# A gated recurrence and a squared-ReLU layer in one program: another order of the opening, shorter zero products, a later third step of each weight conversion, narrower state products in the last blocks

## The chip, the core and the metric

The kernel runs on one core of one Trainium2 chip. The metric is the device time of one execution in microseconds; lower is better. A core has a matrix engine (TensorE, PE in the profile, with its weight loads listed as PEld), a vector engine (VectorE, DVE), a scalar engine (ScalarE, ACT), GpSimd (POOL) and a queue engine (SyncE, SP) that here issues all transfers. Each engine works through its own list of instructions in order and waits on semaphores for the others.

## What is computed

Per head and batch, a state of 48 x 48 is decayed row by row with alpha and takes up the outer product of k and v; q reads it. The results, side by side by head, go through two matrix products with a squared ReLU between them. All is float32, except the two weight matrices, which arrive as float64 bit patterns.

```python
batch, n_heads, seq, head_dim = (4, 8, 768, 48)
for t in range(S):
    state = alpha[:, :, t, :, None] * state + np.einsum('bhd,bhe->bhde', k[:, :, t], v[:, :, t])
    y[:, :, t] = np.einsum('bhd,bhde->bhe', q[:, :, t], state)
x = y.transpose(0, 2, 1, 3).reshape(B * S, H * D)      # 3072 x 384
h = np.maximum(x @ w_in, 0.0)                          # w_in 384 x 2048
return (h * h @ w_out).astype(np.float32)              # w_out 2048 x 384
```

## The kernel before

**Blocks and groups.** The sequence is cut into 6 chunks of 128 steps; a block is one chunk of one batch, all 8 heads: 24 blocks, numbered chunk by chunk, so that blocks 0 to 3 are the first chunk of the four batches. Four blocks make a group of 512 rows for the two layers: 6 groups.

**One block of the recurrence.** `ln` takes the logarithm of alpha (ScalarE), `cs` sums the logs along the chunk with a triangular matrix (TensorE), `eb` and `ei` take the exponentials of the sums and their negatives (ScalarE), `mq` and `mk` scale q and k with them (VectorE). q and k are turned (`qT`, `kT` in the first group, `turn` later, L351 and L567) and copied to SBUF by ScalarE (`qc`, `kc`). `scores` (L410) multiplies turned k and q in four quarters of 64 x 64; `masked` (L421) copies the causal part. `state_sums` (L438) multiplies k and v, the k times v products; `sums_copied` (L451) adds the first half's sums to the state, and `next_state` (L467, L468) makes the new state and decays it by the last row of the exponentials, which `lt` brings into columns (L334, L341; later a transfer does it). y is made for two blocks at a time from the states and from the masked scores (L390, steps `ya`, `yb`), and `ev` (L605) copies it from PSUM into x, some copies on VectorE (those listed under `evd`), the rest on ScalarE. Each head has 48 columns in a slot of 64; the pad columns of k are zero, so the k times v product with 64 columns of k writes zeros into rows 48 to 63 of its slot.

**The layers.** `ffn_in` (L908) multiplies w_in and x for one of 16 columns blocks j of the hidden layer, in float32, which counts as two TensorE instructions a product in the trace; a whole unit has 3 products with 512 rows, a half unit (`ha`, `hb`) 3 with 256, the first or the last two blocks of the group. From group 1 on, most products are made in three passes with rounded parts of the operands (L715 and L798), whose splits VectorE and ScalarE prepare. After the last pass of a hidden column block the squared ReLU is made in one of three kinds, chosen by j modulo 4 from a string of letters: A (three operations on ScalarE), M (two on ScalarE, one on VectorE), D (one on ScalarE, two on VectorE).

**Weights.** w_in and w_out come in 8 slices each of 768 KB (w0, w1 and so on). A slice is converted in seven operations: two on VectorE (`convert_first`, L163 and L167), two on ScalarE (`convert_middle`, L177 and L180), three on VectorE (`convert_second`, L188, L192, L195). Four raw slices can be held. A transfer of q, k, v or alpha is 192 KB.

**The order.** The scheduler keeps the order in which the program records its operations on each engine. The opening is a written list of words in `AT['first']`, run one by one (`ln0` is the step `ln` for block 0; `load2a` loads alpha of block 2, `weights0` the next raw slice; `first0`, `middle0`, `second0` convert slice 0). Before it, `AT['pre']` lists the first six loads. `warm` and `zeros` are TensorE products with zeros that nobody reads. After the list, the units of the layers are laid in a row, each with a cost in plan units, and events (conversions, steps of later blocks, splits) are put between them at due times from `AT` (`weave`, the last lines). In `attention`, the due times of a pair of blocks follow from one number per pair in `AT['g0']`, `AT['g1']` and `AT['g']`.

Of the kernel before, what the change touches and what calls it, by code (L numbers as in the profile page):

```python
# [9 lines left out]
FP32 = mybir.dt.float32  # L10
# [3 lines left out]
ALU = mybir.AluOpType  # L14
# [1 line left out]


GB = 4
AT = {'later': (0, 0, 5, 4, 0, 1, 1), 'evs': 0.5, 'lead': 4, 'post': 3, 'w_first': (46.75, 40.5, 50.75), 'wstep': 1.4, 'w_in_at': 2.25, 'w_in_by': 3.6, 'room1': 22, 'room': 24, 's0': 4, 'ahead': 6, 'late': 2, 'xs': 0.05, 'g0': ((-0.25, 4, False, True, 25.5), (22.25, 6, True, True), (28.25, 8, True, False)), 'sc0': (2.45, 2.35, 2.35), 'g1': ((4.5, 8, False, 16.25), (14.25, 10, True), (34.75, 12, True)), 'g': ((2.075, 6, True), (14.25, 8, True)), 'g1x': 52.0, 'gx': 48.25, 'g0x': 55.75, 'k0': 2, 'h0': 17, 'k1': 4, 'h1': 0, 'h1by': 2, 'evs0': 0.5, 'tp': 'ADMD', 'tp1': 'ADAD', 'split': 8, 'o0': (47.5, 46.75), 'o1': (), 'o2': (22.0, 26.25, 25.25, 38.5, 39.75, 35.0), 'str1': 19.5, 'ga': 9.75, 'gb': 12.5, 'cv0': 0.875, 'pre': '0a 1a 0q 0k 1q 1k', 'cp': (), 'evd': ((0, 1, 0), (0, 1, 2), (2, 0, 2), (2, 1, 0), (2, 1, 1), (2, 1, 2), (2, 1, 3)), 'first': 'ln0 warm0 ln1 cs0 zeros3 ei0 mk0 eb0 mq0 kT0 cs1 load2a qT0 kc0 load0v eb1 qc0 sc0 mq1 ei1 ln2 weights0 qT1 am0 qc1 kv0 mk1 load1v first0 kT1 us0 kc1 lt1 sc1 load2q load2k kv1 load3a am1 cs2 eb2 us1 ei2 middle0 ya0 yb0 load2v mk2 ln3 mq2 qT2 qc2 kT2 load3k cs3 ep00 ep01 load3q ep02 load3v kc2 lt0 weights1 sc2 eb3 kv2 second0 ei3 ep03 zeros3 first1 weights2 lt2 middle1 ha0 load4q mk3 mq3 qT3 am2 kT3 qc3 kc3 ha1 sc3 lt3 st0 kv3 load4k second1 am3 us2 ha2 us3 load4a ya2 first2 yb2 weights5 ep20 ep21 weights3 ha3 weights6 ep22 ep23 weights4 middle2 second2 st3 st2 hb2 st1 load4v hb3 hb0 hb1'}


RUN = {0: 128, 32: 32, 64: 64, 96: 32}
# [3 lines left out]
def kernel(  # L26
# [12 lines left out]
    nc = tc.nc  # L39
    B, H, S, D = q.shape  # L40
    C = 128
    NCH = S // C
    NP = H // 2
# [4 lines left out]
    G = 64 - D  # L48
# [19 lines left out]
    s_t = [s_all.pop(0) for _ in range(B)]  # L68
# [8 lines left out]
    NW = 8  # L77
# [21 lines left out]
    def tile_of(x, n):  # L99
        return lent.get((x, n), tiles[x][n % len(tiles[x])])  # L100
# [4 lines left out]
    given, owner = set(), {}  # L105
# [37 lines left out]
    half = {}  # L143
# [35 lines left out]
        )  # L179
        nc.scalar.activation(out=w, in_=lo, func=AF.Copy, scale=2.0**-52, bias=1.0)  # L180

    def convert_second(i):
        if moe_w_in.dtype == FP32:
            return
        need(("mid", i))
        given.add(("w", i))
        w, lo, hi, power, upper = half.pop(i)
        nc.vector.scalar_tensor_tensor(  # L188
            out=power, in0=hi, scalar=0x80000000, in1=power,
            op0=ALU.bitwise_and, op1=ALU.bitwise_or,  # L190
        )
        nc.vector.scalar_tensor_tensor(  # L192
            out=w, in0=upper, scalar=2.0**-20, in1=w, op0=ALU.mult, op1=ALU.add
        )
        nc.vector.tensor_tensor(out=w, in0=w, in1=power.bitcast(FP32), op=ALU.mult)  # L195

    for word in AT["pre"].split():
        load(int(word[0]), word[1:])
# [25 lines left out]
    last = consts.tile([128, 4, NP], FP32, name="last")  # L224
# [18 lines left out]
    blk = [{} for _ in range(NBLK)]  # L243
# [17 lines left out]

    SPLIT = AT["split"]

# [98 lines left out]
    def copied(x, n):  # L362
        t = blk[n][f"{x}s"] = work(f"{x}s", 2 if x == "k" else 4)
        copy = nc.vector.tensor_copy if f"{x}{n}" in AT["cp"] else nc.scalar.copy
        copy(out=t, in_=blk[n].pop(f"{x}T"))
# [8 lines left out]
    def zeros(n):  # L374

        ps = bank(n, "zeros", (2 * NP, 64))
        for _ in range(3):
            nc.tensor.matmul(  # L378
                out=ps[:, 0:NP, :], lhsT=s_t[3].rearrange("a p d -> a (p d)")[:, 0:128],
                rhs=s_t[3], start=True, stop=True,  # L380
            )

    def y_begin(n):
# [16 lines left out]
    HALF = [slice(0, 64), slice(64, C)]  # L400
# [29 lines left out]
    def state_sums(n):  # L430
        need(("v", n), ("kb", n))
        given.add(("free", "k", n))
        ps = two[n]
        for p in range(NP):
            for e in range(2):
                first = (2 * p + e) * D
                for h in range(1 if n // B == NCH - 1 else 2):
                    nc.tensor.matmul(  # L438
                        out=ps[h][64 * e : 64 * (e + 1), 1, p, G:64],
                        lhsT=tile_of("k", n)[HALF[h], 2 * p + e, :],  # L440
                        rhs=tiles["v"][n % NV][HALF[h], first : first + D],
                        start=True, stop=True, skip_group_check=True,
                    )

    def sums_copied(n):

        if n >= 3:
            need(("st", n - 3), ("y", n - 3))
        ps = two.pop(n)
        u = blk[n]["u"] = u_all[n % 3]  # L450
        nc.vector.tensor_tensor(  # L451
            out=own(u), in0=own(ps[0][:, 1]), in1=own(s_t[n % B]), op=ALU.add
        )
        blk[n]["kv1"] = own(ps[1][:, 1])

    def own(x):
        return x[:, :, G:64]

    def next_state(n):
        blk[n]["s"] = s_t[n % B]  # L460
        given.add(("st", n))
        if n // B < NCH - 1:
            need(("last", n))
            s_all.append(s_t[n % B])
            s_t[n % B] = s_all.pop(0)
            s, last = own(s_t[n % B]), last_t[n % 4].unsqueeze(2).to_broadcast([128, NP, D])
            nc.vector.tensor_tensor(out=s, in0=blk[n].pop("kv1"), in1=own(blk[n]["u"]), op=ALU.add)  # L467
            nc.vector.tensor_tensor(out=s, in0=s, in1=last, op=ALU.mult)  # L468

    def dep(later, earlier):  # L470
        tc.add_manual_dep(
# [113 lines left out]
    def ev(n, ps=tuple(range(NP))):  # L585
# [12 lines left out]
        for p in ps:  # L598
            for e, f, end in ((1, 2 * p * D + 32, 2 * (p + 1) * D), (0, 2 * p * D, (2 * p + 1) * D)):
                copy = nc.vector.tensor_copy if (n, e, p) in AT["evd"] else nc.scalar.copy  # L600
                r = 64 * (e ^ p % 2)
# [28 lines left out]
    here, todo, room = {}, [], [22]  # L630
# [8 lines left out]
    late = [False]  # L639
# [20 lines left out]
    def diff_w(w, p):  # L660
# [7 lines left out]
        for x in "ld":  # L668
            t = made.pop((x, w, p))
            if w == "i" or p >= NW - AT["k0"] or (x == "l" and p >= NW - AT["k1"]):  # L670
                here[x, w, p] = t
        pump()

    def prepare(at, w, p):
        step = AT["wstep"]
        fs = (cast_w, rest_w, diff_w)
# [289 lines left out]
    first = AT["first"]  # L966
# [127 lines left out]
    units.append((0, ended, (0,)))  # L1094
    base = [0]
    cv0 = AT["cv0"]
    events = [(3.4 * i + cv0, next_weights, (3 + i,)) for i in range(-3, 2 * NW - 3) if ("mid", 3 + i) not in given]
    events += [(3.4 * i + cv0 + 1.5, convert_second, (3 + i,)) for i in range(-3, 2 * NW - 3) if ("w", 3 + i) not in given]
    events += [(0, load, (GB + 1,)), (1.0, load, (GB + 2, "k"))]
    for p, at in enumerate(AT["w_first"]):  # L1100
        events += prepare(at, "i", p)
# [7 lines left out]
    for g in range(1, NG):  # L1109
# [11 lines left out]
        if g == 1:  # L1121
            m = len(AT["w_first"])
# [4 lines left out]
            n = min(AT["k0"], AT["k1"])  # L1127
# [34 lines left out]
```

## Time and profile before

| what | value |
|---|---|
| median of 3 runs | 523.61 us (522.96 to 523.86) |
| the profiled execution: its own time | 523.38 us |
| its span | 521.6 us |
| TensorE busy | 511.3 us (98%) |
| VectorE busy | 363.7 us (70%) |
| ScalarE busy | 304.8 us (58%) |
| mean granted TensorE clock | 0.997 |
| transfers | 102.35 MB, 196 GB/s on average |

The span is the profiled execution from its first to its last instruction; the time of the execution has 1.8 us more around it. Busy shares are averages over stages with different limits: the opening, in which attention of the first blocks and the first weight slices arrive, is bound by other things than the stream behind it. "Idle before" in a line is the time that the engine stood still just before these instructions, with what ended most of it. The chain of waits follows the end of the program back from instruction to what released it. The mean duration of a small TensorE product (221 ns) is its latency; several run at once, so the pace is read from the length of a whole piece.

### The profile page before, as it was taken

To read this page: it belongs to the slowest core of one execution; us is meant where nothing else is said; L and a number is where in the kernel's file an instruction comes from. 1 tells how busy PE (TensorE), PEld (TensorE's weight loads), DVE (VectorE), ACT (ScalarE), POOL (GpSimd) and SP (SyncE) were. 2 spreads that over 40 slices of the span, in tenths; PEclk is the share of its full clock that TensorE was granted. 3 is DMA by queue.
4 is the path that set the end of the run, shared out by engine and by line. 5 is a ranking of instruction groups with operands and counts; after the bars stand their busy time and mean duration, and the time that the engine had idled before them with its cause. 6 is when DMAs were issued, how large, how long until landed. Compare 5 with 4: busy or idle time off the path is not lost.

```text
span 521.6 us, 13021 instructions
## 1 busy us (share of the span) xinstructions
PE 511.3 (98%) x5340; PEld 422.0 (81%) x5340; DVE 363.7 (70%) x628; ACT 304.8 (58%) x649; POOL 5.3 (1%) x29
## 2 busy tenths in 40 slices
PE   8799999999999999999999999999999999999997
PEld 6675455669888669987899988899988899988997
DVE  3577989999886958866587477487465386363861
ACT  4658895577778834585773275872275683164620
POOL 4000000000000000000000000000000000000000
PEclk9899999999999999999999999999999999999999
DMA  9997878556587675999784678864683544699201
GB/s 185 185 284 157 235 190 185 115 130 237 187 234 173 199 218 165 286 310 246 179 239 153 214 246 221 231 197 142 207 284 128 175 129 152 208 389 299 74 1 60
DMA packets 139323, 102.35 MB, mean 196 GB/s; under 512 B 109808, under 2 KB 112896, under 8 KB 139264
## 3 DMA queue, kind: packets, MB, share of 16 engines
q1 hardware_dynamic: 139264, 101.52, 68.4%
q8 instruction: 42, 0.69, 0.6%
q14 instruction: 17, 0.14, 0.1%
HBM read 84.17 MB, written 17.33 MB: 195 GB/s over the span
## 4 chain that ended last, share of the span: by engine, by line
PE 94%; SPq 2%; ACT 1%; DMA 1%; DVE 1%; issue 0%; POOLq 0%; DVEq 0%
PE o L798 41%; PE h L715 32%; PE h L908 7%; PE y L390 5%; PE sckv L410 2%; PE T L567 2%; PE sckv L438 2%; SPq L119 1%; DMA v_in<-in_v_dram 1%; PE cs L280 1%; PE cs L283 1%; PE cs L284 1%; PE zeros L378 1%; DVE x L605 0%; ACT x L605 0%
## 5 line engine op out<-in xcount | busy, mean ns | idle before, releaser
L715 PE MATMUL h<-xd,wd 128*128 128x512 f32 x240 | 68.4, 397 | 0.5 <-issue 0.5
L715 PE MATMUL h<-xa,wb 128*128 128x512 f32 x240 | 68.6, 394 | 0.0
L715 PE MATMUL h<-xl,wl 128*128 128x512 f32 x240 | 67.7, 390 | 0.0
L637 DVE TENSOR_TENSOR hid<-h,hid 128x512 f32<-128x512 f32 x40 | 27.6, 689 | 54.0 <-PE h L715 53.9
L605 ACT COPY x<-y 16x256 f32<-16x256 f32 (+2 forms) x133 | 46.9, 365 | 22.6 <-PE y L390 18.8
L732 ACT ACTIVATE h<-h 128x512 f32<-128x512 f32 x40 | 23.3, 582 | 56.6 <-PE h L715 56.3
L798 PE MATMUL o<-wb,ha 128*128 128x384 f32 x160 | 54.4, 340 | 0.0
L798 PE MATMUL o<-wd,hd 128*128 128x384 f32 x304 | 53.7, 334 | 0.0
L798 PE MATMUL o<-wl,hl 128*128 128x384 f32 x160 | 53.6, 335 | 0.0
L798 PE MATMUL o<-w_out,hid 128*128 128x384 f32 x160 | 53.6, 489 | 0.0
L715 PEld LDWEIGHTS h<-xl,wl 128*128 128x128 f32 x240 | 45.1, 188 | 9.8
L798 PEld LDWEIGHTS o<-wd,hd 128*128 128x128 f32 x304 | 52.8, 188 | 0.0
L715 PEld LDWEIGHTS h<-xd,wd 128*128 128x128 f32 x240 | 44.1, 188 | 9.9 <-issue 0.9
L715 PEld LDWEIGHTS h<-xa,wb 128*128 128x128 f32 x240 | 44.4, 188 | 9.4
L798 PE MATMUL o<-wb,hx 128*128 128x384 f32 x144 | 48.3, 336 | 0.0
L798 PE MATMUL o<-wl,hx 128*128 128x384 f32 x144 | 48.2, 334 | 0.0
L798 PEld LDWEIGHTS o<-w_out,hid 128*128 128x128 f32 x160 | 30.0, 190 | 19.7
L908 PE MATMUL h<-x,w_in 128*128 128x512 f32 (+1 forms) x120 | 43.7, 514 | 0.9 <-DVE x L605 0.8
L730 ACT ACTIVATE hid<-h 128x512 f32<-128x512 f32 x40 | 24.2, 604 | 33.8 <-PE h L715 33.7
L908 PEld LDWEIGHTS h<-x,w_in 128*128 128x128 f32 x120 | 22.1, 190 | 18.4 <-issue 14.3
L690 ACT ACTIVATE ha<-hid 128x512 fp32r<-128x512 f32 x40 | 25.5, 640 | 15.7 <-PE o L798 9.0
L637 DVE TENSOR_TENSOR osb<-o,osb 128x384 f32<-128x384 f32 x24 | 12.9, 556 | 26.6 <-PE o L798 25.4
(114 smaller groups left out, 886.4 us busy)
## 6 DMA issues: line engine op xcount, KB each, us to landing
wd<-do SPq DMA_DIRECT2D x36, 384.0 KB
wl<-lo SPq DMA_DIRECT2D x34, 384.0 KB
wl<-li SPq DMA_DIRECT2D x32, 384.0 KB
wd<-di SPq DMA_DIRECT2D x32, 384.0 KB
raw<-in_moe_w_in_dram SPq DMA_DIRECT2D x8, 768.0 KB
raw<-in_moe_w_out_dram SPq DMA_DIRECT2D x8, 768.0 KB
v_in<-in_v_dram SPq DMA_DIRECT2D x24, 192.0 KB
out_dram<-osb SPq DMA_DIRECT2D x24, 192.0 KB
```

The lines of the kernel that those rows point to most:

```text
L390: ins = nc.tensor.matmul(out=ys[e][64 * half : 64 * half + D + G * e, m % 2, p // 2, t], lhsT=lhsT, rhs=rhs, start=(half, e) not in seen, ...
L410: nc.tensor.matmul(out=ps[e][HALF[h], 0, p, :], lhsT=ks[rows, p, HALF[h]], rhs=qs[rows, p, HALF[h]], start=True, stop=True, skip_group_che ...
L438: nc.tensor.matmul(out=ps[h][64 * e : 64 * (e + 1), 1, p, G:64], lhsT=tile_of("k", n)[HALF[h], 2 * p + e, :], rhs=tiles["v"][n % NV][HALF[ ...
L567: nc.tensor.transpose(out=ps[h][:, i, p, :], in_=rows[HALF[h], 128 * p : 128 * (p + 1)], identity=ident[HALF[h], HALF[h]],)
L605: copy(out=x[kk][to : to + m, t : t + 2], in_=blk[n]["y"][e][r : r + m, :, p // 2],)
L637: nc.vector.tensor_tensor(out=o, in0=x, in1=z, op=op)
L690: nc.scalar.activation(out=a, in_=x, func=AF.Copy, scale=NEAR * E)
L715: nc.tensor.matmul(out=acc["h", j], lhsT=here[w, "i", p][:, kk, jj * 128 : (jj + 1) * 128], rhs=x_parts[x][:, kk], start=start and kk == 0 ...
L730: nc.scalar.activation(out=hid[j], in_=x, func=AF.Copy, scale=E)
L732: nc.scalar.activation(out=x, in_=x, func=AF.Copy, scale=1.0 + E)
L798: nc.tensor.matmul(out=acc[t][:, 0:DM], lhsT=lhs[:, t * C : (t + 1) * C], rhs=rhs, start=start, stop=stop, skip_group_check=True,)
L908: nc.tensor.matmul(out=ps, lhsT=w[:, kk, c0 : c0 + 128], rhs=xT[g][kk][:, cols], start=(kk == 0), stop=(kk == KM - 1),)
```

## The change

Nearly all is in the table of numbers and words. The order of the opening list differs, and with it the order of the first loads: before, alpha, q and k of blocks 0 and 1, alpha 2, v0, slice 0, v1, q2, k2, alpha 3, v2, k3, q3, v3, slices 1 and 2; after, the same six with block 1's alpha and q ahead of block 0's, alpha 2, slice 0, v0, v1, alpha 3, k3, q2, k2, q3, slice 1, v3, slice 2, v2. The zero products become 2, 2 and 1 of 128 columns instead of 3 and 3 of 256. The number of h units before the turning of blocks 4 and 5 grows by one. The conversion of a slice is cut after its second VectorE step of the last three; the third is recorded behind the next slice's first two. From block 16 on, the k times v products take 48 columns of k, and the VectorE operations on their results are done in two ranges of 48 rows instead of one of 128.

```diff
-AT = {'later': (0, 0, 5, 4, 0, 1, 1), 'evs': 0.5, 'lead': 4, 'post': 3, 'w_first': (46.75, 40.5, 50.75), 'wstep': 1.4, 'w_in_at': 2.25, 'w_in_by': 3.6, 'room1': 22, 'room': 24,
+AT = {'m48': 16, 'cvs': 3.3, 'cv1': 0.75, 'cv2': 0.05, 'later': (0, 2, 0, 0, 1, 0, 2), 'evs': 1.0, 'lead': 4, 'post': 3, 'w_first': (44.75, 42.5, 51.75), 'wstep': 0.9, 'w_in_at': 2.25, 'w_in_by': 3.8, 'room1': 22, 'room': 26,
...
-'xs': 0.05, 'g0': ((-0.25, 4, False, True, 25.5), (22.25, 6, True, True), (28.25, 8, True, False)), 'sc0': (2.45, 2.35, 2.35), 'g1': ((4.5, 8, False, 16.25), (14.25, 10, True), (34.75, 12, True)), 'g': ((2.075, 6, True), (14.25, 8, True)), 'g1x': 52.0, 'gx': 48.25, 'g0x': 55.75,
+'xs': 0.7, 'g0': ((2.25, 4, False, True, 28.25), (24.25, 6, True, True), (27.75, 8, True, False)), 'sc0': (2.35, 2.35, 2.35), 'g1': ((4.5, 8, False, 15.25), (14.25, 10, True), (34.25, 12, True)), 'g': ((1.7, 6, True), (13.5, 8, True)), 'g1x': 51.5, 'gx': 46.25, 'g0x': 55.25,
...
-'h0': 17, 'k1': 4, 'h1': 0, 'h1by': 2, 'evs0': 0.5, 'tp': 'ADMD', 'tp1': 'ADAD',
+'h0': 16, 'k1': 4, 'h1': -2, 'h1by': 2, 'evs0': 0.55, 'tp': 'DDAD', 'tp1': 'AADD',
...
-'cv0': 0.875, 'pre': '0a 1a 0q 0k 1q 1k', 'cp': (), 'evd': ((0, 1, 0), (0, 1, 2), (2, 0, 2), (2, 1, 0), (2, 1, 1), (2, 1, 2), (2, 1, 3)),
+'cv0': -0.5, 'pre': '1a 0a 1q 0k 0q 1k', 'cp': ('q2a', 'q0a', 'q3a', ...), 'evd': ((0, 0, 0), (0, 0, 1), (0, 0, 2), (0, 1, 2), (0, 1, 3), (2, 0, 1), (2, 0, 2), (2, 0, 3), (2, 1, 0)),
-'first': 'ln0 warm0 ln1 cs0 zeros3 ei0 mk0 eb0 mq0 kT0 cs1 load2a qT0 kc0 load0v eb1 qc0 sc0 mq1 ei1 ln2 weights0 qT1 am0 qc1 kv0 mk1 load1v first0 kT1 us0 kc1 lt1 sc1 load2q load2k kv1 load3a am1 cs2 eb2 us1 ei2 middle0 ya0 yb0 load2v mk2 ln3 mq2 qT2 qc2 kT2 load3k cs3 ep00 ep01 load3q ep02 load3v kc2 lt0 weights1 sc2 eb3 kv2 second0 ei3 ep03 zeros3 first1 weights2 lt2 middle1 ha0 load4q mk3 mq3 qT3 am2 kT3 qc3 kc3 ha1 sc3 lt3 st0 kv3 load4k second1 am3 us2 ha2 us3 load4a ya2 first2 yb2 weights5 ep20 ep21 weights3 ha3 weights6 ep22 ep23 weights4 middle2 second2 st3 st2 hb2 st1 load4v hb3 hb0 hb1'
+'first': 'ln0 cs0 eb0 warm0 ln1 zeros2 ei0 mq0 load2a mk0 weights0 kT0 cs1 kc0 qT0 ei1 load0v qc0 sc0 eb1 lt1 load1v mq1 load3a mk1 qT1 am0 ln2 kT1 load3k qc1 kc1 kv0 load2q first0 sc1 load2k load3q kv1 us0 am1 us1 cs2 weights2 middle0 load3v ya0 ln3 ei2 eb2 second0 lt0 mq2 yb0 zeros2 ep00 mk2 qT2 weights5 kT2 cs3 ep01 ep02 qc2 load2v kc2 ep03 ei3 eb3 sc2 first1 mk3 mq3 lt2 am2 middle1 second1 ha0 load4v weights6 qT3 st0 qc3 zeros1 kT3 kc3 weights3 ha1 kv2 sc3 kv3 first2 us2 am3 us3 load4k ha2 middle2 st2 ya2 yb2 first3 ep20 ep21 ep22 ep23 st1 ha3 lt3 middle3 load4q load4a second2 hb0 st3 second3 weights4 weights1 hb3 hb2 hb1'
...
-        for _ in range(3):
+        for _ in range(n):
             nc.tensor.matmul(
-                out=ps[:, 0:NP, :], lhsT=s_t[3].rearrange("a p d -> a (p d)")[:, 0:128],
-                rhs=s_t[3], start=True, stop=True,
+                out=ps[:, 0 : NP // 2, :], lhsT=s_t[3].rearrange("a p d -> a (p d)")[:, 0:128],
+                rhs=s_t[3][:, 0 : NP // 2], start=True, stop=True,
...
-                        out=ps[h][64 * e : 64 * (e + 1), 1, p, G:64],
-                        lhsT=tile_of("k", n)[HALF[h], 2 * p + e, :],
+                        out=ps[h][64 * e : 64 * e + m, 1, p, G:64],
+                        lhsT=tile_of("k", n)[HALF[h], 2 * p + e, 0:m],
...
+    def rows_of(n):
+        return [slice(0, D), slice(64, 64 + D)] if n >= AT["m48"] else [slice(0, 128)]
...
+            for r in rows_of(n):
+                nc.vector.tensor_tensor(out=s[r], in0=kv[r], in1=u[r], op=ALU.add)
+            for r in rows_of(n):
+                nc.vector.tensor_tensor(out=s[r], in0=s[r], in1=last[r], op=ALU.mult)
...
+    def convert_third(i):
...
+        w, power = half.pop(i)
         nc.vector.tensor_tensor(out=w, in0=w, in1=power.bitcast(FP32), op=ALU.mult)
...
+            events += [(at + AT["cv1"], convert_second, (i, False)), (at + cvs + AT["cv2"], convert_third, (i,))]
```

In `state_sums`, `m` is 48 from block 16 on and 64 before; `sums_copied` is cut in the same way as `next_state`. In the opening list, `second` still runs all three operations. The new entries of `cp` have a letter behind the block number, and the program asks for names without one.

## The prediction

> **What bounds the kernel now.** I read the chain of waits first, then its opening in order of time, then TensorE and its granted clock by single microseconds, then VectorE in order of time, then the groups by shape.
>
> ```profile
> PE 94%; SPq 2%; ACT 1%; DMA 1%; DVE 1%; issue 0%; POOLq 0%; DVEq 0%
> ```
>
> TensorE is the chain. From 40.45 us to the last output step at 518.17 its long pieces are all TensorE's, the only other one shown a gap of 0.51 us, so there a cheaper instruction on another engine is worth nothing. The opening differs:
>
> ```profile
> 9.09 6.08 DMA v_in<-in_v_dram
> 15.22 0.68 PE sckv L438 x32
> ...
> 22.33 0.59 ACT ks L365
> ...
> 24.58 2.64 PE zeros L378 x6
> ...
> 36.92 0.42 DVE x L605
> ...
> 40.45 7.16 PE h L908 x26
> ```
>
> Start, length, what: the chain waits for the second v tile until 15.2, for a ScalarE copy queued behind five x copies at 22.3, runs 2.64 us of zero products, and from 36.9 to 40.4 waits for the copies that turn y of blocks 2 and 3 into x. Only at 40.45 does the unbroken stream begin.
>
> ```profile
> 22.00:23.00 1.00, 0.03 (x4) 1.00 0.23 33
> 23.00:24.00 1.00, 1.00 (x52) 0.72 0.81 147
> 24.00:25.00 1.00, 1.00 (x25) 0.50 0.95 319
> 25.00:26.00 1.00, 1.00 (x4) 0.50 1.02 348
> 26.00:27.00 1.00, 1.00 (x4) 0.57 1.02 393
> ```
>
> Stretch, length, busy time (instructions), granted clock, DMA share, GB/s: after the gap the clock is half from about 23.3 to 26.6; the zero products fall into that (six in 2.64 us, 440 ns each, against 280 for the six at 5.95).
>
> ```profile
> 26.84 0.56 DVE L163 TENSOR_SCALAR power<-raw 128x768 uint32<-128x768 uint32 x1 [2.06 <-DMA raw<-in_moe_w_in_dram]
> ```
>
> VectorE waits 2.06 us here for the second weight slice (w1).
>
> ```profile
> L438 PE MATMUL sckv<-v_in,k_in 64*64 64x48 f32 x672 | 15.6, 221 | 0.6 <-DMA v_in<-in_v_dram 0.6
> ...
> L390 PEld LDWEIGHTS y<-am,v_in 64*48 64x48 f32 x384 | 12.7, 120 | 4.3 <-issue 3.8 <-POOLq L507 0.5
> ...
> L451 DVE TENSOR_TENSOR us<-sckv,s 128x192 f32<-128x192 f32 x24 | 8.3, 349 | 0.0
> ```
>
> Count, busy us and mean ns: the costs of the k times v products, of a 48-column weight load, and of one state operation.
>
> **What stays.** The built orders hold the same TensorE work: 780 h, 992 o, 736 score and k times v, 736 y, 320 turning products each; only zeros go from 6 to 5, of half the width. After the opening the same pieces follow one another, a few of them up to eight products earlier or later. So the time moves by when the stream begins, by cheaper k times v products, and by new stalls.
>
> **The opening.** *To the first y.* Alpha of block 1 is now loaded ahead of block 0's, q of block 1 ahead of block 0's, and w0 ahead of v0. Ahead of the second v stand the same bytes, so it lands near 15.2 again. v0 now has 8 small tiles (0.197 MB) and one slice (0.786 MB) up to its end, 2.36 MB; the windows before reach that sum at 13.1, and tiles were usable 1.0 to 2.2 us after their bytes had passed: 14.4. TensorE's order is now v0's products, scores 1, v1's products, sums of logs 2, then y: 14.4 + 4 x 0.65 = 17.05, against 16.74 before. With y (2.55) and the last-row products moved into it (0.45), y ends at 20.05 (19.27 before): 0.8 us lost so far.
>
> *To the second y, VectorE.* Its second state sum comes at about 17.45. Then w0's last three operations, now ahead of the x copies (starts 0.87, 0.98 and 0.88 apart): 20.2; q2, k2 (0.47 each) and seven x copies (0.43) to 24.2, against 25.2 where ScalarE ended them before. w1 is now behind 14 small tiles and w0, before behind 16: 4.33 MB, passed at 24.65, usable at 25.7 (26.84 before). From there: first two of w1 0.94, k3 and q3 0.94, mask copies 0.68, last three of w1 2.73, state 0.66, first two of w2 0.94, then 1.38 for the two sums and masks: 34.0.
>
> *The same, TensorE.* The first h half needs x at 24.4 and runs to 25.9; 27.0 at half clock. q3's turning waits for VectorE until 27.6; with the single zero product and k3's it ends at 28.75, the second h half at 30.2. v2 has moved behind both slices, 5.5 MB as w2 was before: passed at 27.9, usable at 28.9 to 30.1, so just in time. v2's products, scores 3, v3's products (1.9) end at 32.1, h half three at 33.6, y (1.9) at 35.5. The two chains meet, as y's later heads alone need the 34.0. The zeros taken away (2.64 us in this stretch) pay for themselves because h no longer stands behind them.
>
> *To the stream.* Seven x copies remain on VectorE (3.02 us before for seven), five on ScalarE (1.9): 35.5 + 3.05 = 38.55, where before 40.4. The last last-row product group, before y then, now lies in this wait. **Gain 1.9 us.** Bounds: with w1 there by 24.2 and v2 by 28.9 the stream begins at 37.4 (3.0); with w1 at 26.9, v2 at 30.1 and a full half-clock window on TensorE (3.4 us, up to 1.2 not covered) at 39.9 (0.5). I take 1.9, since the lags seen lie mostly near the lower end.
>
> **48 columns.** For blocks 16 to 23 the load of the k times v product shrinks from 64 to 48 columns: 134 to 139 ns against 120 in the rows. 32 products take 0.45 us on the chain, 14.1 ns each; 16 of the last chunk 0.38. If that pace follows the columns, 0.11 us a block, 0.9 in eight; if issue sets it (scores with 64 moving columns take 0.46 too), nothing. I take **0.4**. The rows 48 to 63 of the sums are no longer written, so VectorE's operations on them are split in two: 8 for the sums, 8 for the states more, 16 x 0.35 = 5.6 us. Their cover is VectorE's idle third:
>
> ```profile
> 300.00:340.00 40.00, 40.00 (x597) 33.08 (x598) 25.92 (x52) 29.04 (x69) 0.00 (x0) 1.00 0.81 227
> ```
>
> busy 25.9 of 40. Without cover a block's PSUM banks come free 0.35 to 0.7 us later, at worst 8 x 0.7 = 5.6; TensorE never waited there, so I price nothing. [...]
>
> **Weight conversion.** The third operation goes behind the next slice's first two, at a spacing of 3.3 for 3.4 units. It fills VectorE's wait for ScalarE (0.53 us a slice, 6.4 us over nine) and moves nothing on TensorE by itself; slices were ready 2 us or more before use. But q and k for the next pair queue behind it. Behind the x copies at 38.55 stand two states (1.3) and two slices' last three (5.5): w3 done at 45.4. From there three slices of 3.9, the next one's first two (0.95) and two of its last (1.85), four scalings (2.0) and some 1.4 of waits behind ScalarE's queue put q5 at 63.3. TensorE, with one more h unit (2.58) ahead of the turning (61.77 before), begins it at 62.45 and needs q5 after three quarters of its 1.15, at 63.3: no slack, so I take 0.2 lost, and 1.5 if VectorE slips. **Other moves**, priced at nothing: the 16 squares of kind M become kind D (VectorE +11 us, ScalarE -9.5, spread over 300 us with a third of VectorE idle); the splits of x are spread out, so that at two layer ends the last differences follow the last output sums: about 220.6 against a need at 220.5, within what I can tell. The new cp names match no key, so those copies stay on ScalarE.
>
> **Sum.** Against the profiled 523.4 us (span 521.6): -1.9 - 0.4 + 0.2 = -2.1, **521.3**. The median of the runs is 523.6, 0.2 above.
>
> **Rivals.** (a) The opening moves less: VectorE becomes its bound, since w0's and w1's last operations stand ahead of x copies and sums. It speaks for it that the VectorE chain above has hardly a gap from 17.5 to 34; against it that the old one ended at 34.8. At 1 us later: 522.3. (b) *Slower*: v2, moved behind two slices, lands late. From its landing T the stream begins at T + 0.65 x 2 + 0.6 + 1.5 + 1.9 + 3.05 = T + 8.35; the gain is gone at T = 32.0, and with the other terms it is slower by over 0.2% from T = 33.3. For it: DMA fell to 26 and 33 GB/s in single microseconds (17, 22), and each transfer waits for the one eight before. Against it: the bytes passed by 27.9. At 34.2: 525.3. (c) The clock: shorter zeros and a wait for the later alpha 0 after only three warm-up products leave a second half-clock stretch; 3.4 us cost 1.7 of TensorE work, less some 0.5 of waits: +1.2 on a busy stretch, 522.5; two of them 523.7, so 523.0. For it: 1.44 us of gap sufficed before, and my chain has up to 1.7 before q3's turning. Against it: what follows that gap waits for VectorE and v2 anyway. [...]
>
> **How the numbers follow.** Forecast 0.63 (520.0 to 522.4), (a) 0.15, (b) 0.13, (c) 0.09. 0.2% is 1.05 us, about what a measurement of this kernel tells from no change. Faster: 0.63 + 0.11 + 0.03 = 0.77; same: 0.03 + 0.04 + 0.01 = 0.08; slower: 0.01 + 0.12 + 0.02 = 0.15. The range runs from the early stream with the full column gain and small change (about 519.3) to 524.0, leaving out most of (b).
>
> **What would show it.** Right: the h stream unbroken from 38 to 39; y of blocks 2 and 3 ending at 35 to 36; the last x copies on VectorE; k times v of blocks 16 on at 11 to 14 ns a product; no TensorE wait over 0.5 us after 45. Wrong: a wait on v_in before the k times v products at 29 or later by over 1 us (b); half clock beyond one window after 16 (c); a turning waiting for q_in by over 1 us at 62; or the stream at 40 or later.

## The result and the profile after

The changed kernel takes 528.12 us (526.85 to 529.00 in six runs), the kernel before, on the same chip, 523.38 (522.53 to 523.86): a ratio of 1.009, interval 1.0073 to 1.0107. It is slower by 0.9%, where the prediction had 521.3 us and a range up to 524.0. The profiled execution of the changed kernel took 528.73 us, its span 526.6.

First the page of the changed kernel: the packets that bring instructions (queue, kind: packets, MB, share of 16 engines), and the chain of waits by engine.

```profile
q8 instruction: 42, 0.69, 0.6%
...
PE 93%; DVE 3%; issue 1%; ACT 1%; DMA 1%; SPq 1%; DVEq 0%; ACTq 0%; POOLq 0%
```

The chain is TensorE's as before, but "issue", 0% before, has 1%: time in which an engine waited for nothing that the profile shows. The opening of the chain in order of time (start, length, what) says where:

```profile
9.48 1.12 PE kT L359 x4
...
13.41 0.69 PE sckv L418 x32
...
18.68 0.93 PE y L398 x41
19.61 1.64 issue
21.25 0.57 PE y L398 x18
...
33.34 1.06 PE h L924 x4
34.40 2.60 issue
37.00 1.16 PE h L924 x2
38.16 1.95 PE y L398 x63
...
41.08 0.42 DVE x L621
...
44.29 9.73 PE h L924 x32
```

The stream starts at 44.29, not at 40.45 as before, 3.84 us later. TensorE stops twice in the middle of a piece: 1.64 us within the first y, and 2.60 us after four of the six instructions of the third h half (in this kernel h of the opening is L924, y L398, scores L418, k times v L447). In neither place does the profile show a transfer, a semaphore or an engine that it waits for. What follows the second stop is also slow (stretch; busy time and instructions of PE, PEld, DVE, ACT, POOL; granted clock, DMA share, GB/s):

```profile
36.00:37.00 1.00, 0.00 (x0) 0.00 (x0) 0.72 (x2) 0.00 (x0) 0.00 (x0) 1.00 1.04 366
37.00:38.00 1.00, 1.00 (x2) 0.44 (x2) 0.00 (x0) 0.00 (x0) 0.00 (x0) 0.55 0.59 219
38.00:39.00 1.00, 1.00 (x35) 0.91 (x38) 0.00 (x0) 0.77 (x3) 0.00 (x0) 0.50 0.16 51
...
40.00:41.00 1.00, 0.87 (x37) 0.73 (x33) 0.00 (x0) 0.64 (x1) 0.00 (x0) 0.75 0.00 0
```

The granted clock falls to a half as TensorE resumes and stays there for 3.4 us, so y of blocks 2 and 3 takes 2.9 us (38.16 to 41.06) and not 1.9.

From the stream on, the two kernels run alike to 301 us. Between the starts of the third and the fourth three-pass layer the changed kernel needs 80.49 us (301.14 to 381.63), the one before 79.26 (297.45 to 376.71); over the whole stream it loses 1.2 us. The chain there:

```profile
327.10 0.77 DVE am L429 x2
...
328.54 0.36 DVE s L482
...
328.92 0.37 DVE s L482
...
330.08 0.70 DVE hid L653
...
330.82 3.24 PE h L731 x13
```

Here, and between 45 us and the last output step only here, the chain runs through other engines: each state operation is there twice, the first VectorE operation of a squared ReLU of kind D (`hid`, which reads h) stands behind them, and TensorE's next h piece waits 0.80 us for it.

### The profile page after: what moved, and what is told of

Same layout as the page of the kernel before. It is cut to its first block, busy times and chain, and to the rows that moved or that the text cites. A ratio compares the mean times of both kernels' runs of the same rounds, so it can differ in the third digit from the quotient of the medians.

```text
span 526.6 us, 13059 instructions
## 1 busy us (share of the span) xinstructions
PE 512.8 (97%) x5338; PEld 421.6 (80%) x5338; DVE 378.2 (72%) x663; ACT 296.7 (56%) x630; POOL 5.3 (1%) x29
## 4 chain that ended last, share of the span: by engine, by line
PE 93%; DVE 3%; issue 1%; ACT 1%; DMA 1%; SPq 1%; DVEq 0%; ACTq 0%; POOLq 0%
PE o L814 40%; PE h L731 30%; PE h L924 8%; PE y L398 5%; PE sckv L418 2%; PE T L583 2%; PE sckv L447 2%; PE cs L288 1%; DMA q_in<-in_q_dram 1%; SPq L119 1%; PE kT L359 1%; DVE x L621 0%; PE cs L291 0%; PE cs L292 0%; PE qT L359 0%
## 5 line engine op out<-in xcount | busy, mean ns | idle before, releaser
L746 ACT ACTIVATE hid<-h 128x512 f32<-128x512 f32 x56 | 33.8, 604 | 81.9 <-PE h L731 80.3
L653 DVE TENSOR_TENSOR hid<-h,hid 128x512 f32<-128x512 f32 x56 | 38.5, 689 | 42.4 <-PE h L731 38.0
L621 ACT COPY x<-y 48x256 f32<-48x256 f32 (+3 forms) x130 | 46.6, 366 | 14.9 <-PE y L398 11.0
L924 PE MATMUL h<-x,w_in 128*128 128x512 f32 (+1 forms) x120 | 44.1, 518 | 2.8 <-issue 2.6
L924 PEld LDWEIGHTS h<-x,w_in 128*128 128x128 f32 x120 | 22.2, 191 | 20.7 <-issue 17.6
L763 DVE SCALAR_TENSOR_TENSOR hid<-hid 128x512 f32<-128x512 f32 x56 | 37.5, 683 | 0.1
L658 DVE SCALAR_TENSOR_TENSOR hl<-ha,hid 128x512 fp32r<-128x512 f32 x40 | 27.4, 686 | 12.2 <-ACT ha L706 12.2
```

What stands on the lines that cost most here:

```text
L621: copy(out=x[kk][to : to + m, t : t + 2], in_=blk[n]["y"][e][r : r + m, :, p // 2],)
L653: nc.vector.tensor_tensor(out=o, in0=x, in1=z, op=op)
L658: nc.vector.scalar_tensor_tensor(out=o, in0=x, scalar=c, in1=y, op0=ALU.mult, op1=op)
L746: nc.scalar.activation(out=hid[j], in_=x, func=AF.Copy, scale=E)
L763: nc.vector.scalar_tensor_tensor(out=h, in0=h, scalar=0.0, in1=h, op0=ALU.max, op1=ALU.mult)
L924: nc.tensor.matmul(out=ps, lhsT=w[:, kk, c0 : c0 + 128], rhs=xT[g][kk][:, cols], start=(kk == 0), stop=(kk == KM - 1),)
```

## The experiments

All ratios are against the kernel before, run beside them on the same chip; its medians were 522.3 to 522.9 us. Fragments of the diff are of the list `first` where not said otherwise.

**The opening and the rest, apart.** open_new is the kernel before with only the new opening (`pre`, `first`, `evd`, `zeros`); open_old is the changed kernel with the old one.

```diff
-'pre': '0a 1a 0q 0k 1q 1k'
+'pre': '1a 0a 1q 0k 0q 1k'
...
-'first': 'ln0 warm0 ln1 cs0 zeros3
+'first': 'ln0 cs0 eb0 warm0 ln1 zeros2
...
```

> The kernel before with only the opening of the changed one (first loads, the written list, the choice of x copies, the shorter zero products); all due times, kinds, 64-column products and whole conversions stay as before. Theory O (the opening alone costs it: in the changed profile the unbroken stream starts 3.8 us later, at 44.3 against 40.45): 3 to 5 us slower than before, 526.5 to 528.5, stream start near 44, TensorE standing still for nothing visible near 19.6 and 34.4. Rival R (the opening only fits the new due times and conversions, and is late because of them): within 1 us of before.

> The changed kernel with the opening of the kernel before, long zero products too; due times, kinds, 48 columns and the later third conversion step stay changed. Theory O: the stream starts near 40.5 and what is left is the 1.2 us that the changed profile loses between 301 and 382: 523.5 to 525. Rival R: 526 or more.

Measured: open_new 525.72 us, 1.0054 (1.0028 to 1.0080); open_old 529.42, 1.0120 (1.0097 to 1.0142). The new opening alone costs some 2.8 us (3.4 by the medians), at the low edge of the 3 to 5 expected, and TensorE in order of time shows the stop in the third h half at the same instruction; in y, which begins at 21.17 there, it shows none (start, length, line, tile; in brackets the idle time before and its cause):

```profile
37.16 0.70 PE L908 MATMUL h<-x,w_in 128*128 128x256 f32 x2 [2.21 <-issue]
```

open_old missed its expectation: it has no such stop, but waits that the kernel before does not have: for q of the next pair (2.1 us, the longest 1.6), w_in (0.8) and alpha (0.6), and half clock for 3.4 us behind them. The new due times do not fit the old opening, so "all but the opening" can't be read from this kernel.

**The 48 columns and the kinds of squared ReLU.** Two entries of the changed kernel's table taken back:

```diff
-'m48': 16
+'m48': 24
...
-'tp': 'DDAD', 'tp1': 'AADD'
+'tp': 'ADMD', 'tp1': 'ADAD'
```

> The changed kernel with 64 columns and undivided VectorE operations in all blocks. In the changed profile a 32-product piece of k times v takes 0.36 us with 48 columns against 0.45 with 64, so about 0.7 us over 8 blocks is given up. Theory S (the divided operations are what lets VectorE fall behind at 330, where TensorE waits 0.8 us for it): that wait goes, and the time stays within 0.5 us of the changed kernel. Rival K (the kinds D are the cause): the wait stays and the time is 0.5 to 0.8 us longer.

> The changed kernel with the kinds of squared ReLU of the kernel before (four A, four M, eight D of sixteen). Theory S: the wait of TensorE for VectorE at 330 stays at 0.3 us or more, time within 0.4 us of the changed kernel. Rival K: the wait goes and the time falls by 0.8 to 1.2 us. Neither touches the opening, whose stream should start at 44 again.

Measured: no48 (the first entry) 527.23, 1.0075 (1.0049 to 1.0101); kinds_old (the second) 528.14, 1.0100 (1.0076 to 1.0124). In no48 the wait near 330 us is gone and that layer takes 79.49 us, 1.0 less; in kinds_old a wait of 0.36 us stays, and the layer takes 79.94. So the wait comes with the 48 columns, that is with the divided VectorE operations that stand in the chain ahead of it; the letters at most lengthen it. The opening's stops stay in both (3.0 and 2.6 us in the third h half).

> The kernel before with 48-column products and divided VectorE operations from block 16 on, nothing else. Theory S (narrow products gain 0.09 us a piece of 32, the divided operations cost only where VectorE is late for a bank): 0.4 to 0.8 us faster if TensorE doesn't wait for VectorE in blocks 16 to 19, and otherwise from no change to 0.5 us slower with a visible wait of h for hid near 325.

before48 is the kernel before with the 48-column code and `m48` 16: 523.45, 1.0005 (0.9985 to 1.0024). Neither gain nor loss can be told: with the old due times no such wait is among TensorE's. Its profile has stops with no named cause instead, of the sort treated next: 1.5 us at 240 (0.5 in the kernel before) and 0.6 in k times v products at 323.

**What are the stops?** The page has 42 packets of 16 KB on the instruction queue, and TensorE has 5,338 products and as many loads: 254 instructions to a packet, or 127 pairs of load and product. The trace of the changed kernel has 512 instructions of TensorE from the first stop to the second, 253 pairs and 6 that wait for semaphores, and two packets began meanwhile (25.2 and 33.9 us): 256 to a packet. So a packet seems to bring the next 126 to 128 pairs. A kernel that puts 40 tiny products, which nobody reads, ahead of the first sums should move the stops by 40 products:

```diff
+        for _ in range(20):
+            nc.tensor.matmul(
...
+                rhs=s_t[3][:, 0, 0:1], start=True, stop=True,
+            )
...
-'first': 'ln0 cs0
+'first': 'tiny0 ln0 cs0
```

> The changed kernel with 20 tiny zero products (40 TensorE product instructions and as many weight loads, 48 columns against one) put ahead of the first sum of logs, where TensorE stands still from 4.0 to 5.3; no buffer, load or operation of another engine moves. In the changed profile TensorE stands still for nothing visible inside y (11 products into its masked part) and inside the third h half (after 4 of 6). Theory F (TensorE has run through the instructions that were loaded and waits for the next 256, which come through the same transfer engines): both stops move 40 products forward in the list, the first to the start of y, 1 to 5 products in, the second into the scores of block 3 ahead of v3's products, within 8 products; their lengths may change. Rival W (a wait on data that the profile doesn't show): they stay at the same products.

```profile
19.70 0.59 PE L406 MATMUL y<-qs,us 48*64 48x64 f32 x25 [0.32 <-issue]
...
25.63 0.68 PE L426 MATMUL sckv<-qs,ks 48*64 48x64 f32 x29 [0.51 <-issue]
...
37.56 0.45 PE L406 MATMUL y<-am,v_in 64*48 64x64 f32 x11 [1.64 <-issue]
```

The stop in y comes now after its first 3 products, where it came after 43: 40 earlier. The next is after 3 of 32 scores of block 2, 126 products on. None is in the third h half; the last of these lies in the masked products of y for blocks 2 and 3, after 53 of 64, 254 products behind the one in the scores, which is two blocks of instructions. The boundary between them, in the scores of block 3, where the second stop was expected, shows none. The place follows the count of instructions, not the operation or its operands. The kernel took 530.15 us in its one run; its y begins at 19.07, 0.46 later than in the changed kernel.

**Does the rest of the traffic set it?** quiet records three loads of block 4 and two weight slices at the end of the list; early4 puts only the loads of block 4 ahead of two slices, and late4 does the opposite to the kernel before. In early4 and late4 the lists of the four other engines stay word for word.

```diff
-us3 load4k ha2
+us3 ha2
...
-middle3 load4q load4a second2
+middle3 second2
...
-weights4 weights1 hb3 hb2 hb1
+hb3 hb2 hb1 weights4 weights1 load4k load4q load4a
```

That is quiet. early4 takes the same three loads out and has, from the changed kernel,

```diff
-ha0 load4v weights6 qT3
+ha0 load4v load4k load4q load4a weights6 qT3
```

and late4, from the kernel before,

```diff
-ha0 load4q mk3
+ha0 mk3
...
-kv3 load4k second1
+kv3 second1
...
-us3 load4a ya2
+us3 ya2
...
-weights3 ha3
+weights3 load4q load4k load4a ha3
```

> The changed kernel with five transfers (k, q and alpha of block 4, and the sixth and seventh weight slice) issued at the end of the opening's list, so that little is in flight from about 31 to 37. Theory F with the transfer load as its cause: the stop in the third h half, 2.6 us in the changed profile, shrinks below 1.3 us, the stop in y (before which nothing changes) stays at 1 to 2 us. Rival: the fetch is late by itself, and the stop stays at 2 us or more. The whole time may be longer, as block 4 comes later.

> The changed kernel with one thing moved: on the transfer queue, k, q and alpha of block 4 stand ahead of the fourth and fifth weight slices (as in the kernel before) and not behind them; the lists of the other four engines are word for word the same. Theory (a block of TensorE's instructions is fetched late because its packets stand behind the many small packets of these three tiles, in flight from 27 to 36 us): at the boundary inside the third h half only slices are in flight, so the stop of 2.6 us there falls below 0.5, the stream starts at 41 to 42 instead of 44.3, and the time falls by 2 to 3.5 us, to a ratio of 1.002 to 1.006 over the kernel before. Rival (any traffic holds the fetch up, or the place in the program alone): a stop of 2 us or more stays there, ratio 1.008 to 1.011. Second rival (the tiles now stand ahead of v2 or the slices and something waits for those): no stop, but a named wait of a microsecond or more takes its place.

> The kernel before with only the order of loads changed, the other way round: q, k and alpha of block 4 stand behind the fourth and fifth weight slices, where the changed kernel has them; the other four engines' lists are word for word those of the kernel before. Theory (the packets of these tiles delay the fetch of TensorE's next block of instructions): counted in blocks of 128 products from the small stop after the 41st product of y, the next but one boundary lies inside the k times v piece of block 3 (near 33 us, after some 21 of 32 products), where the kernel before runs through; with the tiles in flight at 28 to 36 us a stop of 1 to 3 us without a named wait appears there or close by, the stream starts 1 to 3 us later than 40.45, ratio 1.002 to 1.006. Rival (the stop belongs to the new opening's dense order, not to the loads): no stop, ratio 0.999 to 1.001. Second rival: block 4 comes late, a named wait at 47 to 62 us.

quiet, TensorE in order of time:

```profile
33.84 1.56 PE L924 MATMUL h<-x,w_in 128*128 128x256 f32 x6
...
40.91 9.73 PE L924 MATMUL h<-x,w_in 128*128 128x256 f32 x32 [0.21 <-DVE x L621]
...
67.71 0.46 PE L583 MATMUL T<-ident,q_in 64*128 64x64 f32 x8 [1.39 <-DVE q_in L307]
```

The third h half runs through and the stream starts 3.4 us sooner, but block 4 comes late: 1.39 us at its turning, 0.34 at its sums of logs. 527.81 us in one run. The stop in y is gone too, though nothing ahead of it was changed and it was expected to stay: in this execution the scores of block 0 take 1.14 us, at half clock, against 0.69, and y begins at 21.22. So this run alone does not show that the traffic made the difference. early4 keeps block 4 in time:

```profile
17.14 0.81 PE L398 MATMUL y<-qs,us 48*48 48x64 f32 x32
...
31.34 1.86 PE L924 MATMUL h<-x,w_in 128*128 128x256 f32 x6
...
38.88 1.35 PE L924 MATMUL h<-x,w_in 128*128 128x256 f32 x5 [0.21 <-DVE x L621]
```

No stop in the third h half, stream at 38.88, where the prediction had 38.55. Its median is 523.42, the ratio 1.0034 (0.9997 to 1.0071): by the medians 0.8 us above the kernel before, where the changed kernel was 4.7 above it, from three moves on the transfer queue. But two of its ten executions took 530.0. And late4 did not bring a stop to the kernel before: it is at 522.01 us, 0.9987 (0.9972 to 1.0001), with a piece of h at 38.95 that begins at 39.66 in the kernel before. My theory that these tiles' packets by themselves make the stop fell with it; the first rival, that the stop belongs to the new order of the products, held.

**Combinations.** open_early is open_new with early4's order of loads; early4_no48 and three are the changed kernel with early4's order and 64 columns, three with alpha 0 loaded first as well (the diffs are those shown above and below).

> The kernel before (its due times, letters, whole conversions, 64 columns) with the new opening and zero products, and the loads of block 4 ahead of the fourth and fifth slices. If the opening's own gain is what its stream start in the run early4 shows (38.9 against 40.45), and the rest then runs as in the kernel before: 1 to 1.5 us faster than before, ratio 0.997 to 0.9985. If its new opening doesn't fit the old due times: a wait of TensorE or a late block 4 after 45 us, ratio 1.000 or more.

> The changed kernel with the loads of block 4 ahead of the fourth and fifth slices and 64 columns in all blocks. Against early4 it should save the wait for the squared ReLU near 330 us and give up the cheaper k times v products: 0.5 to 1 us less, ratio 0.998 to 1.0015. If the wait at 330 was only moved: the same as early4, 1.002 to 1.004.

> The changed kernel with three things taken back: the loads of block 4 ahead of the fourth and fifth slices, alpha 0 loaded first, 64 columns in all blocks. If the causes found add up (stop in the third h half 2.6, late start up to 1.5, the wait at 330 us 1.1): stream at 39.5 to 41, no wait of TensorE over 0.5 after it, ratio 0.997 to 1.002. If something else of the new order costs time on its own: 1.003 or more.

open_early 524.24, 1.0027 (0.9998 to 1.0055); early4_no48 523.56, 1.0041 (1.0010 to 1.0071); three 524.29, 1.0040 (1.0009 to 1.0071). All three were expected at or near a gain, and none has one. They scatter: of open_early's twelve runs six took 521.1 to 523.4, five of them some 1 us under the kernel before, and six 525.1 to 528.3. The profile caught one of the latter:

```profile
27.32 0.26 PE L334 MATMUL lastT<-ident,b 128*48 128x1 f32 x5 [1.19 <-issue]
...
36.67 0.70 PE L908 MATMUL h<-x,w_in 128*128 128x256 f32 x2 [2.60 <-issue]
```

The loads stand as in early4, and the stop is there again, behind the same product. So the order of the loads shifts the odds, not the rule: of the four kernels with early4's order 17 of 44 runs took over 525 us, of the six with the new opening and the loads late (changed kernel, open_new, no48, kinds_old, warm4, alpha0) 31 of 35. That each of these runs had the stop is not shown, as only one of each is profiled. early4_no48's profile has a stream at 38.73 and ends at 519.9 us, 1.7 below the span of the kernel before; its median does not follow.

**When the packet passes.** Narrow windows of the transfer view show in which half microsecond a 16 KB packet of the instruction queue began (a quarter in the last row); its own time, by its share of the engines, is 0.9 to 1.5 us. Beside it, when TensorE came to the end of its block and when it went on:

```
kernel            packet from   reached   went on   stop
after                18.0        19.61     21.25    1.64
after                33.5        34.40     37.00    2.60
open_early           24.5        26.13     27.32    1.19
open_early           34.0        34.07     36.67    2.60
no48                 32.5        32.45     35.49    3.04
warm4                32.5        31.91     35.36    3.45
early4_no48          29.5        32.29     32.58    0.29
before               28.0     about 33.1      -     none
one_zeros_again     108.5       108.92    111.03    2.11
```

TensorE goes on 2.2 to 3.5 us after its packet has begun, in every row with a stop. In the kernel before the packet began 5 us ahead of its need. The blocks there begin at about 23.8 and 33.1: 9.3 us for a block. In the changed kernel the matching block, with the zeros cut and the waits closed, is 6.6 us (27.8 to 34.4). What delays a packet stays open: from the start of the block before it, in the opening, it took under 1 us at the least (three, at 26.0) and over 7 at the most (warm4, from 25.2).

**A faster start.** warm4 adds one warm-up product to the changed kernel; alpha0 loads alpha 0 first again.

```diff
-'first': 'ln0 cs0
+'first': 'warm0 ln0 cs0
...
-'pre': '1a 0a 1q
+'pre': '0a 1a 1q
```

> The changed kernel with one more warm-up product ahead of the first sum of logs, so that TensorE hardly stands still before 5.3. Theory C (the clock stays at half until about 12.7 because of that gap, and this costs the opening): the first turning takes 0.66 us instead of 1.12, scores 0 start at 12 instead of 13.4, and the time falls by 1 to 1.5 us. Rival: the later stops and the VectorE chain take it back, 0.4 us or less.

> The changed kernel with alpha of block 0 loaded first again, as before; nothing else. Theory: the sums of logs of block 0 start near 4.5 instead of 5.28 and run without the wait of 1.26; TensorE is at full clock by 8 us as in the kernel before, scores 0 start near 11.5 instead of 13.4. But the stop inside the third h half ends when the fetch has landed, and that does not hang on the start: it stays after 4 of 6 products and gets longer, so the stream still starts at 43 to 44.5 and the time gains less than 1 us: ratio 1.007 to 1.01. Rival (the late start runs through to the stream): stream at 42 to 42.8, ratio 1.004 to 1.006.

warm4 527.87, 1.0085 (1.0059 to 1.0112): in its profile block 0's scores start at 12.07, 1.3 us sooner, and the stop in the third h half is 3.45 us long, and two instructions earlier, as the count demands (one of its ten runs took 522.68):

```profile
35.36 1.13 PE L924 MATMUL h<-x,w_in 128*128 128x256 f32 x4 [3.45 <-issue]
```

alpha0 527.86, 1.0097 (1.0082 to 1.0112): block 0's sums start at 4.24, but k comes no earlier, the clock is half from 8.9 to 19.1, and the scores start at 13.56; the stop is 2.22. What TensorE gained ahead of the packet it lost at the packet: block 0's scores 1.3 us sooner in warm4, the stop 0.85 us longer and the time within 0.3 us of the changed kernel's.

**The zeros.** one_zeros is the kernel before without its second group of zero products; it ran twice, the second time for another profile.

```diff
-second0 ei3 ep03 zeros3 first1
+second0 ei3 ep03 first1
```

> The kernel before without its second group of zero products (six instructions, 2.71 us at half clock in its profile); nothing else. Theory (these zeros lie in the time in which the next block of TensorE's instructions arrives and in front of a wait for VectorE, so they cost nothing): the h half starts earlier, the wait for q of block 3 grows by as much, the stream starts where it did, ratio 0.999 to 1.0005. By the prediction's reckoning (TensorE's chain sets the start): stream 1.5 us or more earlier, ratio 0.997. If the fetch is then too late: a stop without a named wait before 34 us and a ratio over 1.001.

> The kernel of one_zeros once more, for a profile: five of its six runs took 525.9 to 527.4, the profiled one 523.6. If the fetch is what makes the others slow: a profile at 526 or more shows a stop without a named wait of 1 us or more before 45, or half clock behind it, in the piece that starts the second block of 128 products after y. If the profile is again at 523 to 524, nothing new.

526.98 us, 1.0067 (1.0046 to 1.0087): to leave out 2.71 us of products that nobody reads makes the kernel 3.5 us slower. The second profile, 527.9 us, shows two causes. Granted clock by stretches (columns as above):

```profile
22.00:23.00 1.00, 0.60 (x38) 0.61 (x40) 1.00 (x2) 0.96 (x5) 0.00 (x0) 0.96 0.40 68
23.00:24.00 1.00, 1.00 (x43) 0.91 (x36) 0.97 (x2) 0.95 (x4) 0.00 (x0) 0.50 0.86 221
...
27.00:28.00 1.00, 0.56 (x2) 0.00 (x0) 1.00 (x3) 1.00 (x2) 0.00 (x0) 0.50 1.12 322
...
32.00:33.00 1.00, 1.00 (x14) 0.35 (x17) 0.40 (x1) 0.22 (x1) 0.00 (x0) 0.50 0.83 270
33.00:34.00 1.00, 1.00 (x52) 0.92 (x44) 0.00 (x0) 0.58 (x2) 0.00 (x0) 0.92 0.93 291
```

From the 0.96 and the 0.92 the clock was half from 22.92 to 33.16: 10.24 us, where the kernel before had it half for one stretch of 3.4. And six products fewer shift every later boundary by six. One of these boundaries now shows a stop, near 109:

```profile
111.03 0.45 PE L390 MATMUL y<-am,v_in 64*48 64x64 f32 x11 [2.11 <-issue]
```

Here scores, k times v and y follow one another, 149 products in 2.44 us (106.48 to 108.92), and the block ends within y. After this stop, too, the clock is half for 3.4 us. The first profile (523.6 us) has a stop of 1.17 at the same place and only one stretch of 3.4 us at half clock, in the opening. The shift itself does not explain the stop: by the count the boundary lies in the same y in the kernel before, six products sooner, and no stop is seen there. Its packet began at 103.5, some 4 us ahead; in the two profiles without the zeros at 105.25 and 108.5. Why it came later is not shown.

**Towards a version that beats both.** ha3_late moves the squared ReLU of the fourth h half behind ScalarE's x copies in the kernel before; late4_ha3 joins it with late4.

```diff
-weights3 ha3 weights6 ep22 ep23
+weights3 weights6 ep22 ep23 ha3
```

> The kernel before with the squared ReLU of its fourth h half moved behind the x copies of ScalarE on ScalarE's list, so that two operations (some 0.5 and 0.65 us) no longer stand ahead of copies that the stream waits for at 36.9 to 40.4; nothing else. Expected: stream 0.3 to 1 us earlier, ratio 0.998 to 0.9995. Rival: the copies on VectorE end last anyway (the chain shows x copies of VectorE at 36.92), ratio 1.000.

> The kernel before with the two moves of the runs late4 and ha3_late together: loads of block 4 behind the fourth and fifth slices, the squared ReLU of the fourth h half behind ScalarE's x copies. If late4's lead (0.9987) is real and ha3_late adds nothing: 0.998 to 0.9995, a version that beats both kernels. If late4's lead was chance: 1.000.

ha3_late 523.03, 1.0005 (0.9988 to 1.0022): the rival held. late4_ha3 522.66, 0.9998 (0.9985 to 1.0012). So late4's lead is within chance, and no version that surely beats the kernel before was found.

## Why the prediction was wrong

**What failed** is the step "The same, TensorE", with "h half three at 33.6, y (1.9) at 35.5" and the stream at 38.55. It took TensorE's own instructions as present whenever their operands are. In its main case it also took the clock as full from the first turning on: the one of k takes 1.12 us (9.48) instead of 0.66, so the step "To the first y" has y at 17.05 where it began at 18.6, and the first stop, 1.64, lies within that y. In early4, which has the same list on TensorE but took that turning in 0.66, y began at 17.14. Set against the profile, the 5.74 us between 38.55 and 44.29 are these: the fourth instruction of the third h half was due at 33.1 (two thirds of 32.1 to 33.6) and ended at 34.40, 1.3 later (what the opening's other waits left of that slow start and the first stop); the stop added 2.60; the half clock behind it made y end 5.56 late, 1.7 more; the x copies took 3.16, not 3.05. The profile of the changed kernel has 42 packets of 16 KB on the instruction queue, and at boundaries in the dense parts TensorE stood still for 0.3 to 3.45 us.

**"The zeros taken away pay for themselves"** was wrong for the kernel before, as one_zeros shows; on the changed kernel it was not tried. That the zeros keep the clock up is not shown: without them half clock lasted 3.4 us in one profile and 10.24 in the other, with them 3.4 in the kernel before and 6.84 in late4_ha3.

**Right in the opening**: v2 was in time (the k times v products of block 2 start at 31.73 without a wait), so rival (b) did not come (that each transfer waits for the one eight before is in the trace of the kernel before: w0, the ninth, issued at 7.94, waits for the semaphore of alpha 0, the first); VectorE did not become the bound, against rival (a); the gain that the order of data and engines would allow is there once the stop is gone (early4: stream at 38.88). The load order did count, but in neither way that I weighed.

**Rival (c)**, the clock, came true in part. The late start at half clock is there (block 0's scores at 13.41, before at 10.37), but not in every execution, as early4 shows, and alpha 0 first did not cure it. The stretch behind the third h half, 1.7 us of work as its price was set, followed the stop and not the wait for alpha 0. Slower by 0.9% was outside all my cases.

**48 columns.** The gain was there and the cover was not. In the chain of the changed kernel

```profile
262.22 0.36 PE sckv L447 x32
```

stands against 0.45 before: 0.09 us for 32 products, nearer to the upper bound of 0.11 than the half that I took. But the 16 more VectorE operations, priced at nothing with "TensorE never waited there", cost 1.0 us net in one layer (80.49 against 79.49 in no48). A 48-row operation takes 351 to 355 ns, one of 128 rows 349 to 358, so halves cost double, and the stretch from 327 to 330 has no idle third: averages over 40 us hid that.

**Weight conversion** and the other moves behaved: the turning of blocks 4 and 5 ran without a wait, for 0.2 priced.

## What to carry to other kernels

This unrolled program had one more input stream, its own instructions: 42 packets of 16 KB. Where the trace shows "issue" in the middle of a piece, count the products between such stops, look for instruction packets in the transfer view, and compare the time that a block lasts (here some 127 products) with the time that its packet needs (here 2.2 to 3.5 us from its beginning until TensorE went on). Closing waits and taking out slow products made a block shorter here, 6.6 us for 9.3, and a stop of 2.60 us followed. An edit that changed nothing but the number of products moved the boundaries behind it (by 40 products in shift, by six in one_zeros), so judge an opening by several runs and not by one profile. And read the cover for added work in the very microseconds where its result is awaited.

## What the runs showed of the hardware

From the beginning of a packet of instructions TensorE took 2.2 to 3.5 us to go on in the eight stops of the table (the packet itself lasted 0.9 to 1.5 of these), more than the 2.1 us that 127 of its smallest products lasted (149 in 2.44 us in one_zeros_again). And transfers were not dense at every stop: in one_zeros_again none moved from 104.0 to 107.2 us, one of 384 KB from then to 108.2, and the packet right behind it, at 108.5; the stop in y was still 2.11. Whether a packet waits for the transfers ahead of it, as this looks, was not shown.

In the opening, from where the clock is recorded (6.4 us in the kernel before, 13.2 in the changed one), half clock lasted 3.41 us in the kernel before (23.45 to 26.86) and twice 3.41 in the changed one (23.44 to 26.86, and 37.10 to 40.51 behind the second stop), with 10.24 us of full clock in between. Behind the stops of open_new, no48, kinds_old and warm4 it lasted 3.4 us too, in open_early 6.82; in the second profile without the zeros it lasted 10.24 (22.92 to 33.16), three times 3.41, and in alpha0 10.2 (8.9 to 19.1). Idle time does not settle when it falls: in one_zeros_again 1.43 us without an instruction (20.96 to 22.39) lay before the fall at 22.92, while behind alpha0's stop of 2.22 us the clock did not fall. Nor did it rise with work alone: in one_zeros_again TensorE was busy throughout from 23 to 27 us and the clock stayed at half. Why half clock lasted 3.4 us in some executions and two or three times that in others, of the same kernel too, stays open.
